# A planned attention and MLP-mixer kernel: parts of a sum planned back to back, and all orders found anew

## The chip, the core and the metric

The kernel runs on one core of a Trainium2 chip. The metric is the device time of one execution in microseconds. Engines are called as in the profile: PE is TensorE, DVE is VectorE, ACT is ScalarE, POOL is GpSimd, SP is SyncE, which here only issues DMAs.

## What is computed

Linear attention (random features, 8 batches, 8 heads, 576 rows, 64 columns a head, 128 features) feeds a mixer block over tokens and channels:

```python
def _attn_ref(q, k, v, omega):
    scale = 1.0 / np.sqrt(np.sqrt(D))
    def phi(x):
        proj = np.einsum('bhsd,md->bhsm', x, omega)
        h = proj - np.sum(x * x, axis=-1, keepdims=True) / 2.0
        h = h - np.max(h, axis=-1, keepdims=True)
        return np.exp(h) / np.sqrt(m)
    q_p, k_p = phi(q * scale), phi(k * scale)
    kv = np.einsum('bhsm,bhsd->bhmd', k_p, v)
    z = np.sum(k_p, axis=2)
    num = np.einsum('bhsm,bhmd->bhsd', q_p, kv)
    den = np.einsum('bhsm,bhm->bhs', q_p, z)[..., None] + 1e-06
    return num / den

def _moe_ref(x, w_tok1, w_tok2, w_ch1, w_ch2):
    xt = x.transpose(0, 2, 1)
    h = np.maximum(xt @ w_tok1, 0.0) @ w_tok2
    u = x + h.transpose(0, 2, 1)
    h2 = np.maximum(u @ w_ch1, 0.0) @ w_ch2
    return u + h2
```

The model width is 512 (8 heads of 64), the token layer has 256 and the channel layer 1536 units. Inputs and output are float32; the matrix products take float16.

## The kernel before

Nothing in this kernel is written in its final order. Each piece of work is a job (an engine, a cost, a key, the jobs it depends on, the buffers it takes and gives back), and a planner written in Python, `Planner.run`, lets the jobs go one by one: of the jobs that are ready earliest on an engine, the one with the smallest key goes first. The times in the plan are the planner's own (costs, `LATENCY`, `MARGIN`). The instructions are issued in the planned order, each engine executes its own in that order, and semaphores hold them to their dependencies. So every key and every planning rule can move work on all engines and in all DMA queues at once.

The keys stand in tables: `KEYS` for all batches, `NEAR` for batches 1 and 2, `HEAD` for the first batch and the loads at the start. `BY` says which evictions go to ACT and which to DVE.

A batch has 512 main rows and 64 tail rows. It passes through these stages (the names are those of the code, the lines those of the profile):

- The loads. Batches 0 and 1 are loaded as they are and transposed on PE (L485, L505). From batch 2 on, POOL's queue casts q and k into scratch memory (L353, L364, L358), and SP's queue reads them back transposed into `qT` and `kT` (L374). POOL's queue also loads `v` (L331) and its tails `vt` (L345). Before some of these loads POOL runs a one-column copy into `junk`, which waits for a buffer to be free or a transpose to have landed (L380 for `kT`, L386 for `uT`, L392 for the sum `u` of batch 1). All of POOL's jobs, the issue of a DMA and the arithmetic alike, go in one order.
- Attention, by pairs of heads: feature products `kp` (L638), `qp` (L652), and those of the tails, `kt` (L546) and `qt` (L611), whose matmuls have 64 rows and go to two halves of the array; exponentials on ACT (L514); a maximum and a reciprocal on DVE (L664, L666); `vs`, the scaled v, on POOL (L671), with `vbd` for the tails (L596); the product `kv` on PE (L684, L691 or L693); the numerators (L720, L722); and their division on DVE (L729, L730).
- Token mixing: `t1` (L759, L760), ReLU, `t2` (L776), and the sum `u` on DVE (L779). SP's queue transposes `u` into `uT` (L784), and once for two batches the tails `ut` into `uTt` (L843, after `htt`, L835). Batch 0 does this on PE instead, in four column blocks (L803 to L825).
- Channel mixing: `c1`, twelve sums of four matmuls each (L854; for batch 0 the first two are split into `c1a` and `c1b`, L860 and L862), each followed by a ReLU on ACT (L874) or DVE (L876); then `c2`, four sums of twelve matmuls (L892), which DVE adds to `u` (L901; for batch 0 a copy, L898, since four small matmuls of L890 bring `u` into the sum). The result goes out by SP's queue (L908). A ninth channel mix does the tails of all batches (stores in L911); its last sum is split into 384 and 128 columns.

A sum of `c2` is planned as three jobs of four matmuls, each of which depends on the one before it:

```python
for part in range(3):
    ...
    prev = add("PE", mm(4, cols.stop - cols.start) + ..., key + 0.5 + 0.5 * (3 * j + part) / 12 + 0.2 * hf, c2,
               deps=[prev, *jr[4 * part : 4 * part + 4], *j_wc2], take=[("bank", n)], ...)
```

A PE job's planned end is its start, its cost and a latency of 0.25 (`LATENCY["PE"]`), and a job that depends on it may start from that end on. PE itself is free at the start plus the cost. There are eight PSUM banks, three buffers each of `qT`, `kT`, `v`, `x`, `u` and `uT`, and two of `vt` and of `r3`, the ReLUs' output.

Of the kernel before, what the change touches and what calls it, by code (L numbers as in the profile page):

```python
# [13 lines left out]
AX = mybir.AxisListType  # L14


KEYS = {"a": -1.349, "as": 0.099, "t": -1.509, "ts": 0.07, "gv": 2.027, "lt": -1.998, "lv": -3.43, "to": -2.341, "tt": 0.635, "ks": 1.094, "km": 0.635, "vs": -0.113, "l1": -0.452, "kt": -0.125}
NEAR = {"1": {"a": -1.426, "as": 0.259, "t": -2.775, "ts": 0.5, "gv": 0.127, "km": -1.859, "vs": -0.397, "kt": 0.24}, "2": {"a": -2.686, "as": 0.0, "t": -0.589, "ts": 0.371, "gv": -1.065, "km": 3.693, "vs": 0.4, "lv": -3.388, "lt": -2.446, "kt": -0.123}}
HEAD = {"kp": [-3.838, -3.822, -3.881, -3.404], "ke": [-2.728, -2.927, -2.827, -2.727], "km": [-4.039, -3.592, -4.221, -2.25], "vs": [-3.448, -3.487, -3.196, -2.472], "qp": [-3.203, -3.403, -3.303, -3.488], "qe": [-3.328, -3.374, -2.153, -3.748], "kv": [-3.407, -3.228, -2.676, -3.133], "ko": [-2.32, -3.035, -3.463, -3.168], "n": [-3.199, -3.47, -3.182, -2.377, -2.999, -3.268, -2.999, -2.899], "no": [-4.124, -3.487, -3.919, -3.144, -3.226, -3.426, -3.126, -2.386], "ktm": -3.643, "kt": -5.305, "kte": -5.022, "qt": -3.759, "qte": -5.587, "kx": [-6.213, -5.658, -5.326, -5.458], "kxo": [-6.855, -7.05, -5.718, -4.783], "ktx": -6.15, "ktxo": -5.912, "qx": [-4.987, -3.488], "qxo": [-4.073, -2.977], "qtx": -4.567, "qtxo": -3.371, "t1": [0.229, -1.008, -0.737, -0.445], "re": [0.072, -0.781, 0.181, -0.024], "ut": [0.162, -0.48, -0.104, -0.341], "uo": [-0.099, -0.259, -0.108, 0.38], "vbd": -8.41, "w1": -9.7, "w1t": -9.38, "w2t": -8.94, "wa": -8.03, "wb": -9.17, "w2": -10.08}
BY = {"kx": "ADDD", "ktx": "A", "qx": "DD", "qtx": "A", "ko": "DADD", "re": "AAAA", "uo": "AADD", "no": "DDADDADD", "r0": "AAAAADAAADAA", "ko1": "DDAA", "r1": "AAAAAAAAAAAA"}  # L20


def key_of(name, b):

    return NEAR.get(str(b), {}).get(name, KEYS[name])

# [11 lines left out]
class Planner:  # L38
# [37 lines left out]
    def run(self):  # L76
# [6 lines left out]
        while any(waiting.values()):  # L83
            choice = None
            for eng, jobs in waiting.items():
                ready = []
                for j in jobs:
                    t = at[eng]
                    ok = True
                    if j.after is not None and j.after.end is None:  # L90
                        continue
                    for d in j.deps:
                        if d.end is None:
                            ok = False
                            break
                        m = self.MARGIN[eng] if d.eng != eng else 0.0
                        if eng == "PE" and self.warm is not None:
                            m = min(m, 0.05)
                        if eng == "PE" and d.wire:
                            m = 0.5  # L100
                        t = max(t, d.end + m)
                    if not ok:
                        continue
                    self.now = t
                    got = []
                    for tag, name in j.take:
                        if (tag, name) in self.held:
                            continue
                        one = self.find(tag, got)
                        if one is None:  # L110
                            ok = False
                            break
                        got.append((tag, one[0]))
                        t = max(t, one[1])
                    if not ok:
                        continue
                    if j.wire and len(lanes[eng]) >= self.LANES:
                        t = max(t, lanes[eng][-self.LANES])
                    key = j.key - (KEYS["ks"] if eng == "PE" and j.rows and last_rows == j.rows else 0.0)
                    ready.append((t, key, j))  # L120
                if not ready:
                    continue
                first = min(r[0] for r in ready)
                t, _, j = min((r for r in ready if r[0] <= first + 1e-6), key=lambda r: r[1])
                if choice is None or t < choice[0]:
                    choice = (t, j)
            if choice is None:
                stuck = [(e, min(js, key=lambda j: j.key).key) for e, js in waiting.items() if js]
                raise RuntimeError(f"no job can go: {stuck}")
            t, j = choice  # L130
            eng = j.eng
            waiting[eng].remove(j)
            if self.warm is not None and eng == "PE":
                if j.heavy:
                    self.warm = None
                else:
                    while t - at["PE"] > 0.3:
                        self.now = at["PE"] + 0.1
                        free = [i for i, at_ in enumerate(self.places["bank"]) if at_ < self.now]
                        if free:  # L140
                            i = min(free, key=lambda i: (self.warmed.get(i, 0), i))
                            self.warmed[i] = self.warmed.get(i, 0) + 1
                            self.warm(i)
                            last_rows = False
                        at["PE"] += 0.43 if at["PE"] < self.COLD else 0.22
                    t = max(t, at["PE"])
            self.now = t
            for tag, name in j.take:
                if (tag, name) not in self.held:
                    i = self.find(tag)[0]  # L150
                    self.places[tag][i] = math.inf
                    self.held[tag, name] = i
            cost = j.cost
            if eng == "PE":
                cost += self.SWITCH if j.rows != last_rows else 0.0
                last_rows = j.rows
            at[eng] = t + cost
            if j.wire:
                wire = max(wire, t + cost + self.BEFORE[eng]) + j.wire
                j.end = wire + self.AFTER  # L160
                lanes[eng].append(j.end)
            else:
                j.end = t + cost + self.LATENCY[eng]
            j.start = t
            j.fn()
            for g in j.give:
                self.left[g] -= 1
                self.freed[g] = max(self.freed.get(g, 0.0), j.end)
                if self.left[g] == 0:
                    self.places[g[0]][self.held[g]] = self.freed[g]  # L170
# [7 lines left out]
def kernel(  # L178
# [247 lines left out]
    def pads():  # L426
# [4 lines left out]

    j_w1 = dma("POOL", HEAD["w1"], 1.3, cost=0.58, fn=lambda: nc.gpsimd.dma_start(
        out=w1m.rearrange("p j t -> p (j t)"), in_=moe_w_tok1[0:SM, :].rearrange("(p j) t -> p (j t)", j=NJ)))
    j_w1t = []
    def load_w1t(o, key):
        j_w1t.append(dma("POOL", key, 0.2, cost=0.58, fn=lambda: nc.gpsimd.dma_start(out=w1t[o * ST : (o + 1) * ST, o, :], in_=moe_w_tok1[SM:S, :]), deps=[j_w1tz]))
    load_w1t(0, HEAD["w1t"])
    j_w2 = dma("POOL", HEAD["w2"], 1.7, lambda: nc.gpsimd.dma_start(out=w2, in_=moe_w_tok2.rearrange("(i p) s -> p i s", p=P)))
    def w2_of(tb, j):
        return w2[:, tb, 0:SM].rearrange("p (c j) -> p j c", j=NJ)[:, j, :]  # L440
    j_wc1 = []
    def load_wc1(i):
        c0 = i * (DC // 2)
        j_wc1.append(dma("POOL", HEAD[("wa", "wb")[i]], (3.9, 4.4)[i], lambda: nc.gpsimd.dma_start(
            out=wc1[:, :, c0 : c0 + DC // 2], in_=moe_w_ch1[:, c0 : c0 + DC // 2].rearrange("(i p) c -> p i c", p=P))))
# [72 lines left out]
    def attention(b, key, step):  # L518
# [12 lines left out]
        n_kt = ("kt", b)  # L531
        kkt, k0 = (key + key_of("kt", b),) * 2 if b else (HEAD["kte"], HEAD["kt"])
        kqt, kqe = (key + 0.1 * step, key + 0.1 * step) if b else (HEAD["qt"], HEAD["qte"])
# [386 lines left out]
    for h0, h1 in ((0, 4), (4, 8)):  # L920
        transposes(1, "k", h0, h1, KEYS["l1"] + 0.1 * h0)
        transposes(1, "q", h0, h1, KEYS["l1"] + 0.1 * h0 + 0.01)
    tail_transposes(1, "k", -0.55)
# [3 lines left out]
    for b in range(B):  # L927
# [6 lines left out]
        if 0 < b < B - 2:  # L934
            touched[b] = touch(b, b + KEYS["to"], uT)
        if b % 2:
            tails.append(token_tail(b // 2, b + KEYS["tt"], r1s[b] + r1s[b - 1], xs[b] + xs[b - 1]))
        channel_mix(b, float(b), uT)
# [37 lines left out]
```

## Time and profile before

| what | value |
|---|---|
| median of 5 runs | 290.04 us (289.78 to 290.77) |
| the profiled execution | 290.04 us, its span 287.7 us |
| granted TensorE clock | 0.997 |
| PE busy | 280.3 us, 97% of the span |
| DVE, ACT, POOL busy | 152.5, 153.6, 93.4 us |
| DMA | 39.59 MB, 138 GB/s on average |
| first and last PE matmul start | 1.20 us, 283.06 us |

The page tells how long each engine was busy and what ended its waits. A matmul's recorded duration holds its way through the array, so the distance from start to start is what counts for a row of matmuls: a group of twelve that is listed with 2.76 us starts its last matmul 2.38 us after its first. The timeline merges neighbours of the same line, and names in brackets what an engine was idle for. In the chain of work that ended last, PE holds 87% of the span; the rest lies almost all in the first 40 us.

### The profile page before, as it was taken

What the parts mean: (1) busy time and instruction counts of PE and PEld (TensorE: products, weight loads), DVE (VectorE), ACT (ScalarE), POOL (GpSimd) and SP (SyncE); (2) the same over time, 40 slices, a digit from 0 to 9 for tenths busy, and PEclk for the clock granted to TensorE, in tenths of its full rate; (3) what the DMA queues carried; (4) which work ended last, traced back from release to release, by engine and by line L of the source; (5) the groups of instructions that cost most, each with busy time, mean ns of one, the idle gap of its engine ahead of it and who ended that gap; (6) DMA issues with size and microseconds to landing.
All of it is one profiled execution on the core that took longest, in us unless ns stands there. A gap on an engine that the chain in (4) does not pass through costs nothing.

```text
span 287.7 us, 5598 instructions
## 1 busy us (share of the span) xinstructions
PE 280.3 (97%) x2186; PEld 141.0 (49%) x2186; DVE 152.5 (53%) x330; ACT 153.6 (53%) x322; POOL 93.4 (32%) x126
## 2 busy tenths in 40 slices
PE   8999989999999999999999999999999999999993
PEld 4575554444544544464445544554455444444442
DVE  3986963556659624774678346834766331031012
ACT  2994872098439554774666646663676402602700
POOL 8994950129015701660256014801230000000000
PEclk9999999999999999999999999999999999999998
DMA  8999999699968899999889964996821043013014
GB/s 191 193 201 192 203 211 181 120 241 129 171 106 214 133 131 187 154 204 186 110 150 178 232 86 106 166 208 115 160 74 39 0 107 115 0 40 124 2 38 108
DMA packets 85721, 39.59 MB, mean 138 GB/s; under 512 B 64384, under 2 KB 80128, under 8 KB 85504
## 3 DMA queue, kind: packets, MB, share of 16 engines
q0 software_dynamic: 34288, 17.45, 44.6%
q1 hardware_dynamic: 50624, 21.01, 35.0%
q10 hardware_dynamic: 784, 0.79, 0.8%
q8 instruction: 17, 0.28, 0.4%
q14 instruction: 8, 0.07, 0.1%
HBM read 35.88 MB, written 16.52 MB: 182 GB/s over the span
## 4 chain that ended last, share of the span: by engine, by line
PE 87%; POOL 6%; DMA 3%; DVE 2%; issue 1%; ACT 0%; DVEq 0%; POOLq 0%
PE bank L892 33%; PE bank L854 30%; PE bank L776 4%; PE bank L759 4%; DMA r<-in_k_dram 3%; PE bank L638 3%; PE bank L652 2%; PE bank L684 2%; PE bank L720 2%; POOL vs L671 1%; PE bank L760 1%; POOL vt L345 1%; POOL r L313 1%; DVE km L664 1%; PE bank L835 1%
## 5 line engine op out<-in xcount | busy, mean ns | idle before, releaser
L874 ACT ACTIVATE r<-bank 128x512 f16<-128x512 f32 x106 | 63.6, 610 | 72.0 <-PE bank L854 71.3
L892 PE MATMUL bank<-wc,r 128*128 128x512 f16 (+2 forms) x444 | 101.5, 374 | 0.0
L854 PE MATMUL bank<-uT,wc 128*128 128x512 f16 x376 | 89.5, 379 | 0.1
L892 PEld LDWEIGHTS <-r 128*128 128x128 f16 x444 | 40.6, 98 | 47.8 <-issue 4.7
L854 PEld LDWEIGHTS <-wc 128*128 128x128 f16 x424 | 39.6, 97 | 42.5 <-issue 0.4
L664 DVE TENSOR_REDUCE km<-kp 128x8 f16<-128x1024 f16 x32 | 38.6, 1206 | 7.9 <-ACT kp L514 7.9
L514 ACT ACTIVATE qp<-bank 128x512 f16<-128x512 f32 x64 | 36.0, 658 | 10.0 <-PE bank L652 10.0
L671 POOL TENSOR_TENSOR vs<-v,vs 128x512 f16<-128x512 f16 x32 | 33.5, 1060 | 15.5 <-DVE vs L666 9.4
L514 ACT ACTIVATE kp<-bank 128x512 f16<-128x512 f32 x64 | 34.6, 646 | 5.9 <-PE bank L638 5.9
L730 DVE TENSOR_TENSOR x<-bank,rc 128x320 f16<-128x320 f32 x62 | 30.5, 492 | 2.1
L901 DVE TENSOR_TENSOR o<-u,bank 128x512 f32<-128x512 f16 x28 | 19.1, 682 | 19.4 <-PE bank L892 19.2
L779 DVE TENSOR_TENSOR u<-x,bank 128x512 f16<-128x512 f16 x28 | 17.4, 682 | 7.9 <-PE bank L776 7.9
L380 POOL COPY junk<-kT 128x1 f16<-128x1 f16 x6 | 1.1, 185 | 56.3 <-DMA kT<-k 56.3
L729 DVE RECIPROCAL rc<-bank 128x5 f32<-128x5 f32 x62 | 11.4, 184 | 14.5 <-PE bank L722 14.3
L767 DVE TENSOR_SCALAR r<-bank 128x512 f16<-128x512 f32 x7 | 4.8, 691 | 24.2 <-PE bank L760 24.2
L596 POOL TENSOR_TENSOR vbd<-vt,vbd 128x512 f16<-128x512 f16 (+1 forms) x7 | 8.2, 1178 | 24.1 <-DVE vbd L587 11.4
L720 PEld LDWEIGHTS <-qp 128*128 128x128 f16 x256 | 12.7, 98 | 5.7 <-issue 0.4
L759 PE MATMUL bank<-x,w1m 128*128 128x512 f16 x56 | 14.4, 380 | 0.0
L720 PE MATMUL bank<-kvsb,qp 128*128 128x65 f16 x256 | 14.0, 194 | 0.0
L684 PE MATMUL bank<-vs,kp 128*128 128x65 f16 x256 | 13.1, 194 | 0.7 <-POOL vs L671 0.7
L684 PEld LDWEIGHTS <-kp 128*128 128x128 f16 x256 | 10.9, 98 | 5.4 <-issue 1.6
L776 PE MATMUL bank<-r,w 128*128 128x512 f16 x56 | 13.4, 380 | 0.0
(109 smaller groups left out, 270.5 us busy)
## 6 DMA issues: line engine op xcount, KB each, us to landing
out_dram<-o SPq DMA_DIRECT2D x32, 256.0 KB, 2.7
q<-in_q_dram POOLq DMA_DIRECT2D x6, 576.0 KB, 6.5
wc<-in_moe_w_ch_dram POOLq DMA_DIRECT2D x4, 768.0 KB, 10.7
k<-in_k_dram POOLq DMA_DIRECT2D x6, 512.0 KB, 9.0
v<-in_v_dram POOLq DMA_DIRECT2D x6, 512.0 KB, 6.3
r<-in_q_dram POOLq DMA_DIRECT2D x4, 256.0 KB, 7.5
v<-in_v_dram POOLq DMA_DIRECT2D x4, 256.0 KB, 7.5
out_dram<-o SPq DMA_DIRECT2D x5, 128.0 KB, 2.3
```

Of the source, the lines that this page charges most:

```text
L514: nc.scalar.activation(out=out, in_=in_, func=AF.Exp, bias=0.0, scale=1.0)
L664: nc.vector.reduce_max(out=mx, in_=kpv, axis=AX.X)
L671: nc.gpsimd.tensor_tensor(out=vs[:, :, 0:D], in0=t_v[place("v", b)][:, hh[0] : hh[0] + 2, :].rearrange("p h (j d) -> p (h j) d", d=D), in1 ...
L684: nc.tensor.matmul(ps[:, i, :], kpv[:, 2 * i + j // 2, j % 2, :], vs[:, i * NJ + j, 0 : D + 1], start=(i == 0 and j == 0), stop=False, ski ...
L720: nc.tensor.matmul(ps[:, k, j * 65 : (j + 1) * 65], st, s[:, i, 0 : D + 1], start=True, stop=True)
L730: nc.vector.tensor_tensor(out=t_x[place("x", b)][:, :, (2 * hp + hs[0]) * D : (2 * hp + hs[0] + n) * D].rearrange("p j (i d) -> p i j d", ...
L759: nc.tensor.matmul(ps, w1m[:, j, tb * P : (tb + 1) * P], x[:, j, :], start=(j == 0), stop=False)
L776: nc.tensor.matmul(ps, w2_of(tb, j), r1[:, tb, :], start=(tb == 0), stop=(tb == NT - 1))
L854: nc.tensor.matmul(ps, wc1[:, db, cb * P : (cb + 1) * P], moving(db), start=(db == 0), stop=(db == ND - 1))
L874: nc.scalar.activation(out=o, in_=bank(n), func=AF.Relu)
L892: nc.tensor.matmul(ps[:, cols], r3[:, cb, j * P : (j + 1) * P], wc2[:, cb, cols], start=(cb == 0), stop=(cb == NCB - 1))
L901: nc.vector.tensor_tensor(out=t_o[place("o", (c, j))][:, cols], in0=uu[:, cols], in1=bank(n)[:, cols], op=ALU.add)
```

## The change

The planner's rule for dependencies changes. Where both jobs are on PE, the later one may start 0.25 before the planned end of the earlier, that is, as soon as PE is free; on the other engines nothing changes:

```diff
-                        m = self.MARGIN[eng] if d.eng != eng else 0.0
+                        m = self.MARGIN[eng] if d.eng != eng else (-self.LATENCY["PE"] if eng == "PE" else 0.0)
```

With it come other keys:

```diff
-KEYS = {"a": -1.349, "as": 0.099, "t": -1.509, "ts": 0.07, "gv": 2.027, "lt": -1.998, "lv": -3.43, "to": -2.341, "tt": 0.635, "ks": 1.094, "km": 0.635, "vs": -0.113, "l1": -0.452, "kt": -0.125}
-NEAR = {"1": {"a": -1.426, "as": 0.259, "t": -2.775, "ts": 0.5, "gv": 0.127, "km": -1.859, "vs": -0.397, "kt": 0.24}, "2": {"a": -2.686, "as": 0.0, "t": -0.589, "ts": 0.371, "gv": -1.065, "km": 3.693, "vs": 0.4, "lv": -3.388, "lt": -2.446, "kt": -0.123}}
+KEYS = {"a": -1.349, "as": 0.099, "t": -1.509, "ts": 0.187, "gv": 2.165, "lt": -2.428, "lv": -3.989, "to": -2.341, "tt": 0.635, "ks": 1.094, "km": 0.303, "vs": -0.113, "l1": -0.452, "kt": -0.062}
+NEAR = {"1": {"a": -1.734, "as": 0.259, "t": -2.775, "ts": 0.45, "gv": -0.056, "km": -2.03, "vs": -0.397, "kt": 0.253}, "2": {"a": -2.686, "as": 0.0, "t": -0.603, "ts": 0.324, "gv": -1.313, "km": 3.931, "vs": 0.571, "lv": -3.347, "lt": -2.872, "kt": -0.122}}
```

In `HEAD` eight entries change: the second of `kv` from -3.228 to -3.257, `kt` from -5.305 to -4.584, the third of `kxo` from -5.718 to -5.723, `ktx` from -6.15 to -5.661, `qtx` from -4.567 to -4.584, the fourth of `t1` from -0.445 to -0.359, the first of `ut` from 0.162 to 0.056, and `w2t` (which no line reads) from -8.94 to -9.78. `BY`, the jobs, their costs and the buffers stay.

In the instructions that this gives, the order on PE is the same up to the end of `c1a` of batch 0 (28.32 us in the profile before); on POOL and SP it is the same up to 34.4 and 44.7 us.

More of the change, by code (lines that the diff above doesn't have):

```diff
@@ L14 @@
 AX = mybir.AxisListType
-KEYS = {"a": -1.349, "as": 0.099, "t": -1.509, "ts": 0.07, "gv": 2.027, "lt": -1.998, "lv": -3.43, "to": -2.341, "tt": 0.635, "ks": 1.094, "km": 0.635, "vs": -0.113, "l1": -0.452, "kt": -0.125}
-NEAR = {"1": {"a": -1.426, "as": 0.259, "t": -2.775, "ts": 0.5, "gv": 0.127, "km": -1.859, "vs": -0.397, "kt": 0.24}, "2": {"a": -2.686, "as": 0.0, "t": -0.589, "ts": 0.371, "gv": -1.065, "km": 3.693, "vs": 0.4, "lv": -3.388, "lt": -2.446, "kt": -0.123}}
-HEAD = {"kp": [-3.838, -3.822, -3.881, -3.404], "ke": [-2.728, -2.927, -2.827, -2.727], "km": [-4.039, -3.592, -4.221, -2.25], "vs": [-3.448, -3.487, -3.196, -2.472], "qp": [-3.203, -3.403, -3.303, -3.488], "qe": [-3.328, -3.374, -2.153, -3.748], "kv": [-3.407, -3.228, -2.676, -3.133], "ko": [-2.32, -3.035, -3.463, -3.168], "n": [-3.199, -3.47, -3.182, -2.377, -2.999, -3.268, -2.999, -2.899], "no": [-4.124, -3.487, -3.919, -3.144, -3.226, -3.426, -3.126, -2.386], "ktm": -3.643, "kt": -5.305, "kte": -5.022, "qt": -3.759, "qte": -5.587, "kx": [-6.213, -5.658, -5.326, -5.458], "kxo": [-6.855, -7.05, -5.718, -4.783], "ktx": -6.15, "ktxo": -5.912, "qx": [-4.987, -3.488], "qxo": [-4.073, -2.977], "qtx": -4.567, "qtxo": -3.371, "t1": [0.229, -1.008, -0.737, -0.445], "re": [0.072, -0.781, 0.181, -0.024], "ut": [0.162, -0.48, -0.104, -0.341], "uo": [-0.099, -0.259, -0.108, 0.38], "vbd": -8.41, "w1": -9.7, "w1t": -9.38, "w2t": -8.94, "wa": -8.03, "wb": -9.17, "w2": -10.08}
@@ new lines @@
+KEYS = {"a": -1.349, "as": 0.099, "t": -1.509, "ts": 0.187, "gv": 2.165, "lt": -2.428, "lv": -3.989, "to": -2.341, "tt": 0.635, "ks": 1.094, "km": 0.303, "vs": -0.113, "l1": -0.452, "kt": -0.062}
+NEAR = {"1": {"a": -1.734, "as": 0.259, "t": -2.775, "ts": 0.45, "gv": -0.056, "km": -2.03, "vs": -0.397, "kt": 0.253}, "2": {"a": -2.686, "as": 0.0, "t": -0.603, "ts": 0.324, "gv": -1.313, "km": 3.931, "vs": 0.571, "lv": -3.347, "lt": -2.872, "kt": -0.122}}
+HEAD = {"kp": [-3.838, -3.822, -3.881, -3.404], "ke": [-2.728, -2.927, -2.827, -2.727], "km": [-4.039, -3.592, -4.221, -2.25], "vs": [-3.448, -3.487, -3.196, -2.472], "qp": [-3.203, -3.403, -3.303, -3.488], "qe": [-3.328, -3.374, -2.153, -3.748], "kv": [-3.407, -3.257, -2.676, -3.133], "ko": [-2.32, -3.035, -3.463, -3.168], "n": [-3.199, -3.47, -3.182, -2.377, -2.999, -3.268, -2.999, -2.899], "no": [-4.124, -3.487, -3.919, -3.144, -3.226, -3.426, -3.126, -2.386], "ktm": -3.643, "kt": -4.584, "kte": -5.022, "qt": -3.759, "qte": -5.587, "kx": [-6.213, -5.658, -5.326, -5.458], "kxo": [-6.855, -7.05, -5.723, -4.783], "ktx": -5.661, "ktxo": -5.912, "qx": [-4.987, -3.488], "qxo": [-4.073, -2.977], "qtx": -4.584, "qtxo": -3.371, "t1": [0.229, -1.008, -0.737, -0.359], "re": [0.072, -0.781, 0.181, -0.024], "ut": [0.056, -0.48, -0.104, -0.341], "uo": [-0.099, -0.259, -0.108, 0.38], "vbd": -8.41, "w1": -9.7, "w1t": -9.38, "w2t": -9.78, "wa": -8.03, "wb": -9.17, "w2": -10.08}
```

## The prediction

> **What bounds the kernel now.** I read the page first (busy time, the rows of 40 slices), then busy time in windows of 30 us, then TensorE's own waits, and only then the timelines of the few places where TensorE stands still.
>
> ```profile
> span 287.7 us, 5598 instructions
> PE 280.3 (97%) x2186; PEld 141.0 (49%) x2186; DVE 152.5 (53%) x330; ACT 153.6 (53%) x322; POOL 93.4 (32%) x126
> PEclk9999999999999999999999999999999999999998
> ```
>
> ```profile
> core 0: us, PE busy (x) PEld busy (x) DVE busy (x) ACT busy (x) POOL busy (x), PEclk, DMA share, GB/s
> 46.00:76.00 30.00, 30.00 (x250) 15.02 (x248) 16.99 (x35) 16.54 (x36) 10.53 (x15) 1.00 1.10 165
> ...
> 256.00:283.00 27.00, 27.00 (x137) 12.76 (x135) 5.27 (x9) 7.16 (x12) 0.00 (x0) 1.00 0.21 64
> ```
>
> ```profile
> PE bank L943 <- DVE mask L423: 1.2, 1, 1.2
> PE bank L684 <- POOL vs L671: 0.7, 1, 0.7
> PE bank L505 <- DMA r<-in_k_dram: 0.6, 1, 0.6
> ```
>
> From 46 us on TensorE is busy in every microsecond at full clock; the other engines are at about half. The last block is the whole list of waits worth a look: the first is the start, the third (24.05 us) lies ahead of the first instruction that the change moves. So the end is set by TensorE's work plus the standstills that are left, and those are small:
>
> ```profile
> 36.06 1.03 PE L854 MATMUL bank<-uT,wc 128*128 128x512 f16 x4
> 37.76 0.40 PE L684 MATMUL bank<-vs,kp 128*128 128x65 f16 x8 [0.67 <-POOL vs L671]
> ```
>
> ```profile
> 32.45 1.95 POOL L596 TENSOR_TENSOR vbd<-vt,vbd 128x1024 f16<-128x1024 f16 x1
> 34.34 1.07 POOL L671 TENSOR_TENSOR vs<-v,vs 128x512 f16<-128x512 f16 x1
> 35.33 1.30 POOL L345 DMA_DIRECT2D vt<-in_v_dram  x2
> 36.63 3.09 POOL L671 TENSOR_TENSOR vs<-v,vs 128x512 f16<-128x512 f16 x3
> 54.25 0.19 POOL L392 COPY junk<-u 128x1 f16<-128x1 f16 x1 [14.53 <-DVE u L779]
> 54.37 0.18 POOL L380 COPY junk<-kT 128x1 f16<-128x1 f16 x1
> 54.49 0.97 POOL L331 DMA_DIRECT2D v<-in_v_dram  x1
> 62.73 0.18 POOL L386 COPY junk<-uT 128x1 f16<-128x1 f16 x1 [7.26 <-DMA uT<-u]
> ```
>
> Four matmuls from 36.06 at 0.216 each end at 36.92; the next starts at 37.76: 0.84 us lost, because POOL made the second `vs` only at 37.7, behind two DMA issues of 1.30. A second loss of 0.23 is at 39.96, a third of 0.14 at 69.40 (again the first `vs` of a batch). All else after 24 us is work.
>
> **The change, part by part.**
>
> *Work on TensorE: nothing.* The built orders hold the same 2186 matmuls with 23 warm-up ones in both. What could change is the number of passes between matmuls of 64 rows (L638, L652, L611, L546, L505) and full ones: a full 512-column matmul takes 216 ns start to start to the next full one and 312 to one of 64 rows, and the way back costs the same 95. I counted 86 passes (those around L835 included) before and 86 after, so the sum is 0 x 95 ns.
>
> *The sums (L892).* In the order before, none of the 37 sums of twelve is unbroken, and a sum stretches over 28.9 matmuls on average; after, 16 are unbroken and the mean is 18.2. Two rules bear on that. Row first: of two adjacent 512-column matmuls of these lines, 629 pairs in the same bank are 216.2 ns apart and 130 in different banks 215.8; and the windows above are full. The Trainium skill (Perfetto Trace Analysis, "Optimizing Tensor Performance") says that independent groups should rotate through the PSUM banks, so that emptying one overlaps the next group's matmuls; that speaks against twelve in one bank. If emptying were laid bare, each of 37 sums would cost VectorE's 0.69 us (L898, L901), some 25 us by the rule. By the row it is 0: the next sum still goes to another bank, and takes 2.59 us. I take 0. The cover is those 2.59 us; gone, it is 0.69 a sum. The twelfth matmul of a sum comes 2.4 us after the first, and needs the last ReLU (ScalarE, 0.60); before, other jobs stood between, now the margin is 1.8 us, enough with ScalarE at 17 of 30.
>
> *Batch 1's attention, 28 to 44 us.* Ahead of the first c2 matmul (44.38 before) stand the same 468 matmuls and 28 passes in both orders. Only the standstills can differ. POOL's two `vt` issues now precede the first `vs`: 34.39 + 1.30 + 1.07 = 36.76 for `vs0`. TensorE's work from c1a's end at 28.32 to the first L684: six c1 5.18, two transposes 0.90, kp 0.44, c1b 0.43, tail transposes and qt 0.24, four passes 0.38: due at 35.89. It waits 0.87. Then L684/L693 0.35, two qp with passes 0.63, one c1 0.86: the second is due at 38.60, and its `vs` is there at 37.8; the third (38.95) is met within 0.1. So 0.84 goes and 0.87 comes: +0.03. The 0.23 (a bank that VectorE empties) stays. First c2 at 44.4 again.
>
> *SP's queue, 44 to 70 us: the one place where something big moves.* The first sum now ends after 12 x 0.216 + 4 x 0.056 = 2.8 us, at 47.2, and its VectorE copy at 47.9. Its store stands in SP's queue ahead of the transposes qT2 and kT2, which before went at once:
>
> ```profile
> 44.68 3.84 SPq L374 DMA_TRANSPOSE qT<-q  x1
> 48.65 2.52 SPq L374 DMA_TRANSPOSE kT<-k  x1
> 54.22 1.75 SPq L784 DMA_TRANSPOSE uT<-u  x1
> 56.01 12.74 SPq L908 DMA_DIRECT2D out_dram<-o  x4
> ```
>
> So qT2 is issued at about 48.45, 3.8 late. By the landings in the trace qT2 took 6.28 from issue (50.96) and kT2 ended 8.62 after qT2's issue (53.30): now 54.7 and 57.1. TensorE needs qT2 at 56.8 (L611, 56.58 before) and kT2 at 59.8: 2 and 2.7 us to spare, nothing lost. uT1, behind them, is issued at 48.45 + 6.5 = 54.95, waits for kT2's packets (to 56.6), and takes the 2.6 us that an undisturbed one took (172.16 to 174.77) and 0.47 to its signal: 59.7. TensorE wants it at 62.78, as before.
>
> Before, it landed only at 62.25, although its last data packet ended at 58.73: 3.52 us of tail, where the other six have 0.45 to 0.48. At 58.35 the packets of the v load (issued at 54.49) had begun, and the completion writes stood behind them to 63.5. Now POOL issues that load after kT2 lands, at 57.2, and its packets start 3.9 later, at 61.1: uT1 should be through. Then `vs0` of batch 2: POOL was at it 5.54 us after waking at 62.73; now POOL is free at about 65.9, v lands at 58.2 + 8.4 = 66.6, `vs0` ends at 67.8, and L684 is due at 69.26: the 0.14 there goes.
>
> *Other moves on POOL and SP.* In batches 5 and 6 the first two `vs` move behind uT's landing and five load issues (0.57 + 1.73 + 0.55 + 1.25 = 4.1 us), in batch 3 the fourth moves behind the last four; in batch 4 one `vt` issue (0.65) moves ahead of three `vs`; one `vbd` moves behind two issues, uTt3's transpose behind one store. Before, the first `vs` of batches 5 and 6 was done 3.9 and 4.1 us before its L684 (145.66 to 149.59, 176.43 to 180.54), and that L684 now stands some 5 us of work further down TensorE's order, so 4.1 is covered with more than 3 to spare; batch 3's fourth had 3.0 (95.73 to 98.71) against 3.5, and moves down by about 2. I cost these at 0; with a cover gone, up to 4.1 a batch.
>
> *The tail.* Before, sums j=2 and j=3 are interleaved, and the last three VectorE operations queue up:
>
> ```profile
> 282.00 1.68 DVE L901 TENSOR_TENSOR o<-ut,bank 128x512 f32<-128x512 f16 x3 [3.20 <-PE bank L892]
> 282.72 2.05 ACTq L911 DMA_DIRECT2D out_dram<-o  x3
> ```
>
> Now j=2 ends 1.3 earlier, so ScalarE's queue issues the 384-column store at 283.2 (not 283.36) and the last at 284.06 (not 284.20): -0.14.
>
> Sum: +0.03 - 0.14 - 0.14 = -0.25. The profiled run is 290.04 (span 287.7 and 2.3 around it), which is also the median of five: 290.04 - 0.25 = **289.8**.
>
> **The rivals.** *Wash* (0.50): the sum above, within 0.4 of 289.8.
>
> *SP's queue strikes (0.30, slower).* One mechanism: the store ahead of the transposes makes uT1 or v late. It decides once v's packets start before uT1's completion writes are out. The Trainium skill (DMA: Bandwidth & Descriptors, "Queues, rings and completion order") says that a DMA engine takes turns between queues a whole packet at a time, typically 9 to 17 descriptors. The v load shows 66 transfers per DMA engine over 5.17 us (58.35 to 63.52), 78 ns each; 9 to 17 of them are 0.7 to 1.3 us (an estimate by that page), uT1 lands by 61.0, and no time is lost. By the row the meeting cost 3.05: uT1 at 62.8 to 65, and POOL's chain from uT1 to L684 (62.25 to 69.40, 7.15) ends at 70.0 to 72.2, +0.6 to +2.8 against 69.40. I take the row: with the rest 290.5 to 292.7, middle 291.3. For it: the next pair of transposes took 10.7 us from issue to landing (71.15 to 81.84), not 8.6. Against: POOL's loads are done at 47.5, so the two transposes have the DMA engines alone.
>
> *The standstill of 0.84 does not come back (0.10, faster).* If TensorE comes later to the first L684, or POOL earlier, up to 0.87 is saved: 288.9. Against: POOL's chain from 32.45 has no slack.
>
> *Scattered waits (0.10, slower).* 469 waits on TensorE in another order, many on banks that ScalarE frees: +0.4 to +0.8, 290.4.
>
> That the plan stays interleaved is excluded by the counts of sums.
>
> **The numbers.** Two tenths of a per cent, 0.58 us, is about what a measurement of this kernel can tell from no change; that puts the bounds at 289.46 and 290.62. Faster: the no-return case and the lower edge of the wash, 0.25. Slower: the queue case and part of the scattered waits, 0.32. Within: 0.43. Likeliest 289.8, alone 289.4 to 290.3; eight times in ten 288.9 to 292.0.
>
> **What would show it.** Right: TensorE busy 30 of 30 in the windows; the wait at 37.76 replaced by one of about 0.9 near 36; qT2 issued at about 48.4; uT1 landed by 60 with a short tail; no wait at 69; the last three VectorE operations apart. Wrong: a wait of TensorE on uT or `vs` between 62 and 72, passes that cost other than 95 ns, or a hole after 76 us.

## The result, and the profile after

The changed kernel takes 288.89 us (median of 31 executions, 288.44 to 290.18) against 289.90 of the kernel before (52 executions, 289.20 to 291.14) beside it: ratio 0.9965, 95% interval 0.9958 to 0.9972. It is faster by 1.0 us. The prediction had said 289.8, a wash. The profiled execution took 289.10 us, with a span of 287.1 us.

Page, windows and TensorE's waits of the changed kernel, the same views as before (in the windows: the window, its length, then for each engine busy us and count; in the waits: us in total, times, longest):

```profile
span 287.1 us, 5605 instructions
...
PE 280.7 (98%) x2186; PEld 141.8 (49%) x2186; DVE 152.5 (53%) x330; ACT 153.6 (54%) x322; POOL 93.7 (33%) x126
...
PEclk9999999999999999999999999999999999999999
```

```profile
46.00:76.00 30.00, 30.00 (x250) 14.98 (x248) 17.17 (x36) 16.56 (x36) 10.70 (x15) 1.00 1.03 186
...
256.00:283.00 27.00, 27.00 (x138) 12.77 (x135) 5.42 (x9) 7.16 (x12) 0.00 (x0) 1.00 0.22 61
```

```profile
PE bank L684 <- POOL vs L671: 0.7, 1, 0.7
PE bank L611 <- ACT qT L509: 0.2, 1, 0.2
```

The reader is to see that the middle of the run looks as before: TensorE is busy in every microsecond from 46 us on and does the same 2186 matmuls, and one wait on `vs` of the old size is left. The third wait of before, on the load of k at 24 us, is not in this execution; the instructions up to there are the same, and in the profiles of this study its idle time is anything from 0 to 0.69 us. So two single profiles can differ by some tenths of a microsecond in their first 30 us without any cause in the change.

The wait on `vs` has moved, and POOL's timeline (start, length, work) shows why:

```profile
36.64 0.40 PE L684 MATMUL bank<-vs,kp 128*128 128x65 f16 x8 [0.73 <-POOL vs L671]
```

```profile
32.34 1.94 POOL L596 TENSOR_TENSOR vbd<-vt,vbd 128x1024 f16<-128x1024 f16 x1
34.22 1.30 POOL L345 DMA_DIRECT2D vt<-in_v_dram  x2
35.52 4.09 POOL L671 TENSOR_TENSOR vs<-v,vs 128x512 f16<-128x512 f16 x4
```

The two `vt` issues now stand ahead of the first `vs` instead of behind it. SP's timeline shows the store of `o0` ahead of the transposes:

```profile
47.90 0.36 SPq L908 DMA_DIRECT2D out_dram<-o  x1
48.31 2.26 SPq L374 DMA_TRANSPOSE qT<-q  x1
50.70 2.13 SPq L374 DMA_TRANSPOSE kT<-k  x1
54.01 1.35 SPq L784 DMA_TRANSPOSE uT<-u  x1
```

And the end. VectorE's last operations stand apart now, 1.3 to 1.9 us of idle time between them, where before the last three came in one block:

```profile
280.46 0.69 DVE L901 TENSOR_TENSOR o<-ut,bank 128x512 f32<-128x512 f16 x1 [1.90 <-PE bank L892]
282.47 0.97 DVE L901 TENSOR_TENSOR o<-ut,bank 128x384 f32<-128x384 f16 x2 [1.32 <-PE bank L892]
```

So the third sum's two stores (128 KB each, one on SP's and one on ScalarE's queue) are issued 1.87 us ahead of the last matmul's end; before, it was 0.57 us. Here are, of the kernel before, the last matmuls and ScalarE's last store in the timelines, and from the DMA view what the last four stores took from issue to landing (KB each, us to landing):

```profile
282.61 0.67 PE L892 MATMUL bank<-wc,r 128*128 128x128 f16 x9
```

```profile
284.20 0.57 ACTq L911 DMA_DIRECT2D out_dram<-o  x1
```

```profile
out_dram<-o SPq DMA_DIRECT2D x1, 96.0 KB, 2.3
out_dram<-o ACTq DMA_DIRECT2D x1, 96.0 KB, 2.9
out_dram<-o SPq DMA_DIRECT2D x1, 32.0 KB, 2.5
out_dram<-o ACTq DMA_DIRECT2D x1, 32.0 KB, 2.4
```

and the same of the changed kernel:

```profile
282.43 0.61 PE L892 MATMUL bank<-wc,r 128*128 128x128 f16 x8
```

```profile
283.65 0.78 ACTq L911 DMA_DIRECT2D out_dram<-o  x1
```

```profile
out_dram<-o SPq DMA_DIRECT2D x1, 96.0 KB, 2.1
out_dram<-o ACTq DMA_DIRECT2D x1, 96.0 KB, 2.4
out_dram<-o SPq DMA_DIRECT2D x1, 32.0 KB, 2.0
out_dram<-o ACTq DMA_DIRECT2D x1, 32.0 KB, 2.2
```

Before, the last matmul ends at 282.61 + 0.67 = 283.28, the last store is issued 0.92 later and takes 2.4: it lands 3.31 us behind the last matmul. After: 283.04, 0.61 later, 2.2 more: 2.76. That is 0.55 us less, all behind TensorE's end.

What else differs between the two: the last matmul ends 0.24 us earlier in this pair of profiles; from the landing to the end of the span it is 0.23 us longer; and the time of an execution outside the profiled span, which each run gives (device time less span), has a median of 2.00 us over the 31 executions, where the kernel before has 2.45 beside the experiments. The four together, -0.24 - 0.55 + 0.23 - 0.45, make -1.0. Of the first, 0.21 lies ahead of the first c2 matmul (44.38 before, 44.17 after), which in other profiles with the early order of before comes anywhere from 43.8 to 44.5; from there to its end TensorE takes 238.90 and 238.87 us. In the medians the span falls by 0.6 us (287.5 to 286.9). The landing and the longer way from it to the span's end make 0.3 of that. The rest fits small standstills of TensorE, which differ from profile to profile: averaged over the profiles of the runs below, those of batch 1 are 1.04 us in nine with the old order there and 0.90 in four with the new one, the bank wait behind them 0.23 and 0.14, the wait at 69 us 0.15 and 0, and a first `vs` at 125 us 0 and 0.16. Together that is -0.2, an estimate from few profiles.

### The profile page after: what moved, and what is told of

Same layout as the page of the kernel before. It is cut to its first block, busy times and chain, and to the rows that moved or that the text cites. A ratio compares the mean times of both kernels' runs of the same rounds, so it can differ in the third digit from the quotient of the medians.

```text
span 287.1 us, 5605 instructions
## 1 busy us (share of the span) xinstructions
PE 280.7 (98%) x2186; PEld 141.8 (49%) x2186; DVE 152.5 (53%) x330; ACT 153.6 (54%) x322; POOL 93.7 (33%) x126
## 4 chain that ended last, share of the span: by engine, by line
PE 92%; DVE 3%; ACT 2%; DMA 1%; POOL 1%; issue 0%; DVEq 0%; POOLq 0%
PE bank L892 33%; PE bank L854 30%; PE bank L776 4%; PE bank L759 4%; PE bank L684 3%; PE bank L720 3%; PE bank L652 3%; PE bank L638 2%; DVE km L664 2%; PE bank L485 1%; ACT kp L514 1%; PE bank L760 1%; DMA omega_nat<-in_omega_dram 1%; PE bank L943 1%; PE bank L835 1%; PE bank L722 1%
## 5 line engine op out<-in xcount | busy, mean ns | idle before, releaser
L874 ACT ACTIVATE r<-bank 128x512 f16<-128x512 f32 x106 | 62.7, 606 | 64.6 <-PE bank L854 64.5
```

Of the source, the lines that this page charges most:

```text
L874: nc.scalar.activation(out=o, in_=bank(n), func=AF.Relu)
```

## The experiments

Ratios are to the kernel before, run beside the experiment on the same chip (its medians were 289.71 to 290.03 us). "Landing" is from the last matmul's end to the last store's landing, in the one profiled execution (with the interleaved last sums and all their stores it is 3.16 to 3.35 in six profiles and 3.85 in e4, with the new order 2.76 to 2.78 in seven); "outside" is the median of device time less span over all timed executions.

| run | us | ratio (95%) | landing | outside |
|---|---|---|---|---|
| before | 289.93 | 1 | 3.31 | 2.45 |
| changed kernel | 288.89 | 0.9965 (0.9958-0.9972) | 2.76 | 2.00 |
| e1 rule for the last mix only | 289.34 | 0.9981 (0.9968-0.9994) | 2.77 | 2.51 |
| e2 changed, last mix as before | 289.42 | 0.9984 (0.9972-0.9996) | 3.22 | 2.03 |
| e3 rule, old keys | 289.15 | 0.9974 (0.9966-0.9982) | 2.76 | 1.98 |
| e4 new keys, old rule | 290.88 | 1.0038 (1.0023-1.0053) | 3.85 | 1.88 |
| e5 before, VectorE +2 | 290.09 | 1.0010 (0.9996-1.0023) | 3.16 | 2.32 |
| e6 before, no third store | 289.28 | 0.9970 (0.9958-0.9983) | 2.78 | 2.23 |
| e7 changed, vt behind vs | 288.45 | 0.9949 (0.9934-0.9965) | 2.76 | 2.38 |
| e8 changed, VectorE +4 | 288.97 | 0.9967 (0.9958-0.9975) | 2.76 | 2.01 |
| e9 as e7, one more copy | 288.35 | 0.9942 (0.9921-0.9964) | 2.78 | 2.44 |
| e10 before, third store by GpSimd | 290.72 | 1.0030 (1.0016-1.0044) | 4.13 | 2.40 |
| e11 rule for the first mix only | 289.40 | 0.9982 (0.9971-0.9994) | 3.35 | 2.12 |
| e12 before, vt behind vs | 288.93 | 0.9965 (0.9951-0.9980) | 3.32 | 2.40 |
| e13 as e7, two more copies | 288.51 | 0.9942 (0.9920-0.9965) | 2.77 | 2.10 |
| e14 before, ScalarE +2 | 289.54 | 0.9987 (0.9977-0.9998) | 3.18 | 2.12 |
| e15 before, SyncE +2 | 289.67 | 0.9996 (0.9986-1.0007) | not in the trace | 2.29 |

### Which part of the change: the tail, the rest, the rule, the keys (e1 to e4)

The job gets a flag, and the rule holds for flagged jobs:

```diff
-                        m = self.MARGIN[eng] if d.eng != eng else 0.0
+                        m = self.MARGIN[eng] if d.eng != eng else (-self.LATENCY["PE"] if eng == "PE" and j.chain else 0.0)
...
+                               deps=[prev, ...], ...); prev.chain = c == B
```

In e1 this stands in the kernel before; in e2, with `c < B`, in the changed one; e3 and e4 swap the tables of keys.

> The kernel before with its own keys; the new rule holds for the last channel mix (c == B) alone. Only TensorE's order in the last sums moves, nothing on another engine. The sum on record gives the tail 0.14 us: 289.8 us against 289.9 of before, ratio 0.9995. A larger tail (the profile pair shows 4.08 us behind the last matmul instead of 4.40): -0.3 to -0.5 us, ratio 0.998 to 0.999. If the tail is a wash and the gain lies elsewhere: ratio 1.000.

> The changed kernel with its new keys, but the rule does not hold for the last channel mix: its sums are interleaved again as before, and everything ahead of 250 us stays as in the changed kernel. By the sum on record it gives back 0.14 us: ratio to before 0.9970. If the tail carries 0.3 to 0.5 us: ratio 0.998. If the tail is a wash: 0.9965.

> The new rule everywhere, with the keys of before. The store of o0 goes ahead of batch 2's transposes, as in the changed kernel, and the tail is the new one; batch 1's attention keeps its order around the 0.84 us standstill. By the sum on record (0.14 for the tail, 0.14 for the wait at 69 us, which goes): -0.28 us, ratio 0.999. If the rule and the early store carry the whole gain: ratio 0.9965. If the new keys carry it: 0.9995 to 1.000, with a new wait somewhere in PE's list.

> The new keys with the old rule: parts of a sum are interleaved as before, SyncE's order is that of before (o0's store behind batch 2's transposes), batch 1's attention starts as in the changed kernel. By the sum on record nothing is left of the gain: ratio 1.000 (the 0.89 us wait on vs stands in for 0.84 us). If the new keys carry the gain: ratio 0.997 to 0.998. If keys found for one rule are harmful under the other: over 1.000, with a wait that neither kernel has.

e1 changes nothing but TensorE's order in the last sums, and brings -0.59 us (interval -0.93 to -0.17). e2 takes exactly that away from the changed kernel and loses 0.53 us (288.89 to 289.42). The "larger tail" holds; 0.14 lies outside e1's interval. The 0.5 us that e2 keeps over the kernel before are not in the landing (3.22 against 3.31), and the time outside the span has 0.42 of them (2.03 against 2.45). e3 shows that the old keys do nearly as well with the new rule. e4 is slower than both kernels, which only its third theory had foreseen: TensorE's timeline of e4 has a hole where before there was none.

```profile
62.09 0.85 PE L638 MATMUL bank<-omT,kT 64*128 64x128 f16 x8
63.05 0.38 PE L854 MATMUL bank<-uT,wc 128*128 128x512 f16 x1
```

The same eight matmuls take 0.40 us in the kernel before. By the profile they waited for banks that ScalarE's exponentials of `kp` had to empty. With the two matmuls of `qp` just ahead, which were held up too, 1.22 us pass from 61.83 to 63.05 for work that takes 0.55 elsewhere in these traces: some 0.7 us lost. Another 0.5 went in the landing (3.85); why the stores took longer there is open. Keys found under one rule don't carry over to the other.

### What in the tail (e6, e10)

e6 leaves out the third sum's two stores, so those rows of the output stay unwritten; in the store of L911:

```diff
-                            (nc.scalar if j >= 2 and i else nc.sync).dma_start(out=..., in_=...)
+                            j != 2 and (nc.scalar if j >= 2 and i else nc.sync).dma_start(out=..., in_=...)
```

> The kernel before, which leaves out the two 128 KB stores of the third sum (j == 2) of the last channel mix; those 128 output rows stay unwritten. Theory that these stores, which before stand 0.57 us ahead of the last four on the same two queues, hold the last four up: the last store lands about 2.76 us behind the last matmul, as in the changed kernel, instead of 3.2 to 3.3: -0.55 us, ratio 0.9981. Rival, only the place in the queues counts and not the transfer itself (the sum on record): -0.14 us, 0.9995. Rival, the shorter end of the changed kernel comes from TensorE's order: 1.000.

e10 lets GpSimd issue them; in the same line:

```diff
-                            (nc.scalar if j >= 2 and i else nc.sync).dma_start(out=..., in_=...)
+                            (nc.gpsimd if j == 2 else nc.scalar if j >= 2 and i else nc.sync).dma_start(out=..., in_=...)
```

> The kernel before, in which GpSimd issues the two 128 KB stores of the third sum of the last channel mix, so that the queues of SyncE and ScalarE hold only the last four; all bytes are still written, at the same time as before. If places and transfers in one queue hold the last stores up: the last store lands near 2.8 us behind the last matmul, -0.5 us, ratio 0.998. If the bytes themselves do (the 16 DMA engines are full): last issue at +0.60 but landing at 3.1 to 3.3: -0.1 us, 0.9995. If GpSimd's own issue is slow (0.6 to 0.9 us for each in this trace) its stores become the last: 1.000 or more.

e6 keeps the interleaved order on TensorE and has the short landing, 2.78, and the gain (-0.75 us, interval -1.2 to -0.5; some 0.2 of it lies outside the span, 2.23 against 2.46 of the kernel before beside it). So it is not TensorE's order as such but the third sum's stores, 0.57 us ahead of the last four, that held those up. e10 falls to a fourth case that none of its theories had: its own stores, which land 1.99 and 3.63 us behind the last matmul, are not the last, but those of the other queues get slower than in any other run.

```profile
282.32 1.16 POOL L911 DMA_DIRECT2D out_dram<-o  x2 [66.71 <-DVE o L901]
```

```profile
out_dram<-o POOLq DMA_DIRECT2D x2, 128.0 KB, 2.8
out_dram<-o SPq DMA_DIRECT2D x1, 96.0 KB, 2.5
out_dram<-o ACTq DMA_DIRECT2D x1, 96.0 KB, 4.0
out_dram<-o SPq DMA_DIRECT2D x1, 32.0 KB, 3.2
out_dram<-o ACTq DMA_DIRECT2D x1, 32.0 KB, 3.5
```

The last four take 2.5, 4.0, 3.2 and 3.5 us from issue to landing instead of 2.3, 2.9, 2.5 and 2.4. ScalarE's last issue was already at +0.65 us, as after the change. A free place in the queues of SyncE and ScalarE is therefore not enough. But e10 moved more than the queue: GpSimd issued its two stores 0.30 us ahead of and 0.28 us behind the last matmul's end, where before both were issued 0.57 us ahead. Whether the later issue, which leaves more of the third sum's bytes under way beside the last four, or GpSimd's queue itself makes them slow was not tried apart.

### The first channel mix (e11)

> The kernel before with its keys; the rule holds for the first channel mix alone (c == 0), the tail is interleaved as before. The store of o0 goes ahead of batch 2's transposes. By the sum on record the wait at 69 us goes and nothing else: -0.14 us, ratio 0.9995. By the rival on record in which SyncE's queue strikes: +0.6 to +2.7 us, 1.002 to 1.009. If the rest of the gain that the tail does not hold lies here: -0.4 us, 0.9986.

The edit is the flag again, with `c == 0`. The profile has no wait at 69 us, and from the first c2 matmul to TensorE's end it is 238.77 us against 238.90 before: the -0.14 of the sum. That wait is gone in all eight profiles with o0's store ahead of the transposes, and is 0 to 0.42 us in the nine others. The measured -0.5 us (interval -0.84 to -0.17) is more, and the table says where most of it is: 0.33 us are missing outside the span.

### Time outside the span (e5, e8, e14, e15)

Sums over a span could not find this part. Each of these runs makes one engine's program longer by a few tiny instructions, off the critical path; e5 and e8 repeat a memset on VectorE, e14 adds one-column exponentials, e15 repeats two 2 KB stores:

e5 (in e8 `range(5)`, and in the changed kernel):

```diff
-    j_mask2 = add("DVE", 0.3, -1.2, lambda: [nc.vector.memset(mask2, 0.0)] + ...)
+    j_mask2 = add("DVE", 0.3, -1.2, lambda: [nc.vector.memset(mask2, 0.0) for _ in range(3)] + ...)
```

e14, ahead of the exponential of `qt`, and e15, behind the store of L908:

```diff
+                [exp(t_qpt[place("qpt", b)][:, ST + e : ST + e + 1], two(n_qt)[e][:, 0:1]) for _ in range(4 if b == 7 and e else 0)]
...
+                        [nc.sync.dma_start(out=rows[i : i + 1], in_=o[i : i + 1]) for i in range(2 if (c, j) == (5, 0) else 0)]
```

> The kernel before with two more memsets of mask2 on VectorE, 60 ns each, at a place where VectorE is not late; nothing else moves. In the runs so far the time outside the profiled span is 2.45 to 2.51 us where VectorE's trace has 447 instructions (before, tail only), 2.0 us where it has 449 (changed kernel, and it without the tail), and the closing drain of VectorE then ends 0.3 us later inside the span. Theory of the instruction streams' length: outside 2.0 us, the drain late, together -0.2 us, ratio 0.9993. Rival, the 0.45 us outside hangs on something else that the change did (SyncE's stream, the order of TensorE): outside stays 2.45, ratio 1.000.

> The changed kernel with four more memsets of mask2 on VectorE where it is not late. Theory of the instruction streams' length: the two 8 KB instruction fetches that lie behind the span's end in the changed kernel move ahead of it; outside 1.9 us and no late drain: -0.2 to -0.35 us, ratio 0.9955 to 0.9960; if a fetch then meets the last stores, as one seems to in the run of new keys with the old rule (landing 0.54 us later), +0.3: 0.997. Rival, the stream's length does nothing: 0.9965.

> The kernel before with four one-column exponentials on ScalarE in batch 7, which make its program two instructions longer (445, waits fall away), as it is in the run with the rule for the first channel mix alone, whose time outside the span was 2.1 instead of 2.45 us; nothing else differs from before. If ScalarE's program length is what counts: outside 2.1 us, -0.3 us, ratio 0.999. If not: 2.45 us and ratio 1.000.

> The kernel before with two 2 KB stores repeated on SyncE in batch 5, which make its program two instructions longer (148), as in the changed kernel and in the run with the rule for the first channel mix alone (TensorE's and VectorE's programs become one longer each). If SyncE's program length counts: outside 2.0 to 2.1 us, -0.3 to -0.4 us, ratio 0.9987. If not: 2.45 us and 1.000.

VectorE's two (e5) take 0.13 us off the outside time and make its last drain late inside the span (1.32 us from the landing to the span's end instead of 1.09); nothing is won. Its four (e8) change nothing in the total. ScalarE's two (e14; four exponentials, but two waits fall away) bring the outside time from 2.43 to 2.12 us with every order as before; the total goes down by 0.17 us only, or 0.13% (0.02 to 0.23%). SyncE's two (e15) give two groups, 7 of 22 executions at 1.85 to 1.92 us and the others at 2.20 to 2.45, with no gain that shows.

The outside time is no constant of one program either. Of 206 executions of the kernel before beside the experiments 27 have 1.98 to 2.17 us and all others 2.28 to 2.60, at median spans that agree within 0.2 us. The changed kernel stays at 1.85 to 2.20 in all of its executions. Kernels whose traces hold the same number of instructions on every engine have nearly the same median: before, e1 and e12 2.40 to 2.51; changed, e2 and e13 2.00 to 2.10; e7 and e9 2.38 and 2.44. So the outside time goes with the make-up of the programs (the change altered it on every engine by one to five instructions) and not with TensorE's order, and two instructions can move it by 0.3 us. By which mechanism is open. In all traces but one the last 8 KB packet of the instruction queue starts behind the span's end, mostly later where the outside time is longer (2.25 us behind it before, with 2.36 outside in that execution; 1.81 after, with 1.98); but in e10 it starts 1.09 behind with 2.43 outside, so this packet alone does not explain it.

### The standstill that was left (e7, e9, e12, e13)

```diff
-                nc.gpsimd.dma_start(out=o, in_=i)
+                (held.append if b == 2 else lambda x: nc.gpsimd.dma_start(out=x[0], in_=x[1]))((o, i))
...
-                )
+                ); [nc.gpsimd.dma_start(out=o, in_=i) for o, i in held if (b, hp) == (1, 3)]
```

This issues the two `vt` loads of batch 2 behind the fourth `vs` of batch 1 and moves nothing else. e7, e9 and e13 are the changed kernel with it, e12 the kernel before. e9 also repeats the copy of L386 in batch 5 (e13 with `3`):

```diff
-            nc.gpsimd.tensor_copy(out=junk[:, b : b + 1], in_=...)
+            [nc.gpsimd.tensor_copy(out=junk[:, b : b + 1], in_=...) for _ in range(2 if b == 5 else 1)]
```

> The changed kernel; GpSimd issues the two loads of batch 2's v tail behind the four vs products of batch 1 instead of ahead of them (0.69 and 0.61 us of issue that stand between vbd and vs0). Theory: these issues are what batch 1's standstill of 0.89 us at 36.6 us waits for: vs0 ends at 35.4 instead of 36.6, the wait goes, and 288.0 us are left, ratio 0.9935. Rival, a next wait (vs1 to vs3, or the bank wait at 41 us grows): 288.3 to 288.6, 0.9945 to 0.9955. Rival, the v tail lands 4 us later (52 instead of 48 us) and vbd of batch 2 waits for it: 288.9 or more.

> The kernel before, with GpSimd's two loads of batch 2's v tail behind the four vs products of batch 1, as in the run with the changed kernel. Theory that the 0.84 us standstill before and the 0.89 us after have one cause, these two issues: the wait at 37.8 us goes, -0.8 us, ratio 0.997 (up to 0.4 us of it may come back outside the span). Rival, before it was the VectorE or ScalarE work ahead of vs1: 1.000.

> The kernel with the v tail's loads behind the vs products, and on GpSimd one more 1-column copy beside the existing one of batch 5, so that every engine has as many instructions as in the changed kernel. In the run without that copy 0.83 us came off the span (286.05 instead of 286.9) and 0.37 us came back outside it (2.375 instead of 2.0). If the lengths of the instruction streams set the time outside: 2.0 us again, 288.05 us, ratio 0.9935. If not: outside 2.4 us and 288.45 us, 0.995.

> The kernel with the v tail's loads behind the vs products, and two more 1-column copies on GpSimd beside that of batch 5. With one more copy GpSimd's program still had one instruction less than in the changed kernel, since a wait fell away; with two every engine's program has exactly as many as there (GpSimd 193, ScalarE 440, VectorE 451, SyncE 148). If the lengths of the programs set the time outside the span: 2.0 us, and with a span of 286.05 us that makes 288.0 us, ratio 0.9935. If not: 2.4 us outside and 288.4 us, 0.9945.

POOL's timeline of e7:

```profile
32.34 1.94 POOL L596 TENSOR_TENSOR vbd<-vt,vbd 128x1024 f16<-128x1024 f16 x1
34.23 4.09 POOL L671 TENSOR_TENSOR vs<-v,vs 128x512 f16<-128x512 f16 x4
38.27 1.30 POOL L676 DMA_DIRECT2D vt<-in_v_dram  x2
```

The wait at 36.6 is gone, and the span's median falls from 286.9 to 286.05 us: the first theory, in the span. But 0.37 us come back outside it. e12 shows that the 0.84 of before and the 0.89 of after have one cause: without these issues ahead of the later `vs` the kernel before runs in 288.93 us, as fast as the changed one, although its wait at 69 us grows:

```profile
68.55 0.40 PE L684 MATMUL bank<-vs,kp 128*128 128x65 f16 x8 [0.26 <-POOL vs L671]
```

e9 had missed its aim: a wait fell away as the copy came in, and the program stayed one instruction short. In e13 all programs are as long as in the changed kernel, and the outside time is 2.10 instead of 2.4 us, near the 2.0 of its first theory. Its total is not lower than e9's, since its median span is 0.4 us longer. Its profile has two waits that e9's lacks: 0.58 us at 28.86 on a load of q, and 0.34 on batch 4's `vs` at 125.2, a place where the changed kernel lost 0.09. The second also comes without extra copies (0.51 in e8), so it is no sign against them; with six executions each the two totals can't be told apart. The versions with this edit are faster than both kernels, at 288.35 to 288.51 us.

## Why the prediction was wrong, step by step

- *Work on TensorE, nothing:* right. 2186 matmuls and full windows in both.
- *The sums, 0 and not 25 us:* right; TensorE's rows show no wait on a bank that VectorE empties beyond the one at 41 us, 0.14 (0.23 before). The rule on rotating banks, which the prediction read against the new order, is kept by it: a sum's twelve matmuls share one bank in both orders, and the next sum goes to another.
- *Batch 1, +0.03:* right in mechanism and size. The wait stands at 36.64 where 36.76 was worked out, and costs 0.89 from start to start where 0.87 was said. That they agree within hundredths is chance: other profiles with the same order there have 0.82 to 1.01, and 0.75 to 1.10 with the old order.
- *SP's queue, -0.14:* right in its result, by a much thinner margin than worked out. qT2 was issued at 48.31 (48.45 predicted), `uT1` landed at 58.41 with a tail of 0.52 behind its last data packet, and the 0.14 at 69 us is gone. The transposes were faster than assumed: their issues took 2.26 and 2.13 us, not 3.84 and 2.52, and kT2 landed at 55.1, not at 57.1. But the rival in which the queue strikes was near; see below the list.
- *Other moves, 0:* right but for 0.09 us at 125.64, again a first `vs`.
- *The tail, -0.14: here the sum failed.* The mechanism was named (the third sum ends 1.3 us earlier, and the last stores no longer queue up), but only the issue of the last store was followed, and that by half. It moved by 0.32 us against the last matmul, not by 0.14: ScalarE's issue of the 384-column store took 0.50 us instead of 0.75, which the sum had kept. And nothing was put down for the time from issue to landing, 2.4 to 2.2 us, though the trace of before had that row: 2.9 us for a store that others took 2.3 for. The term is 0.55 by this pair of profiles, 0.59 (0.17 to 0.93) by e1, and e6 shows that it hangs on the third sum's stores.
- *What the sum had no term for:* the time outside the span, -0.45 us in the medians, of which 0.23 are given back between landing and span's end. The prediction took the 2.3 us around the span for a constant; it goes with the make-up of the programs, and has two groups of values even in the kernel before. Its cause stays open.

SP's queue had less to spare than the sum says. POOL, which waits for kT2, issued the v load sooner too:

```profile
55.39 0.97 POOL L331 DMA_DIRECT2D v<-in_v_dram  x1
58.54 0.18 POOL L386 COPY junk<-uT 128x1 f16<-128x1 f16 x1 [2.18 <-DMA uT<-u]
```

In the trace that load's first packet starts at 57.95, 0.06 us behind `uT1`'s last data packet, where 1.9 us had been worked out (61.1 against 56.6 + 2.6). All the traces bear the rival's mechanism out. In the eight with o0's store ahead of the transposes v's first packet starts 0.05 to 0.46 us behind `uT1`'s last data packet, and the tail (from that packet to the landing) is 0.45 to 0.65 us. In the eight of the old order that have the landing it starts 0.36 to 0.54 us ahead of it, and the tail is 3.4 to 3.75 us. So of the two costs of a meeting that the prediction weighed, the 3.05 us of the row fit the runs, and the 0.7 to 1.3 us do not. Why v's first packet falls just behind each time stays open.

With -0.55 for the tail, and the -0.2 net of the end, the same sum gives -0.25 - 0.41 - 0.22 = -0.9. The rival that named 288.9 us, the standstill that does not come back, met the number by chance: the standstill came back with 0.89 us, and the gain that could be traced lies at the end of the run and outside its span.

## What to carry to other kernels

Where the engines are full, look at what lies behind the last instruction of the full one: follow each last store to its landing, not to its issue, and ask which earlier stores are still under way. A sum that ends early, so that its store is gone before the last one, counts there, even if it costs or saves nothing on the engine. Differences of a few tenths of a microsecond between two programs can lie outside the profiled span; compare device time less span over many executions, and not in one pair, before a cause is looked for inside.

## What the runs showed of the hardware that was not expected

- Two 128 KB stores 0.57 us ahead of the last four on the same queues cost 0.5 us at the end (landing 3.31 us behind the last matmul with them, 2.78 without, e6); issued by GpSimd instead, and later, they cost more (4.13, e10).
- Two more instructions in ScalarE's program changed the time outside the span from 2.43 to 2.12 us, and one more in GpSimd's (e9 to e13, six executions each) from 2.44 to 2.10. In the kernel before it falls into two groups, 1.98 to 2.17 us in 27 of 206 executions and 2.28 to 2.60 in the others.
- A transposing DMA that landed 0.45 to 0.65 us behind its last data packet landed 3.4 to 3.75 us behind it where a 512 KB load's packets had started 0.36 to 0.54 us ahead of that packet.
- SP took 2.15 to 2.72 us to issue a transpose of q where the packets of POOL's queue took under 0.15 of the DMA engines' time meanwhile (2.26 at 48.31 of the changed kernel), and 3.2 to 7.0 us where they took over 0.3 (3.84 at 44.68 and 6.85 at 100.52 of the kernel before). The two go together in all traces; neither was varied by itself.
